# Weight sums stored one stage late, first raw words beside the first layer's last pieces, sums behind Pool's remainders, early differences on VectorE

## The chip, the cores and the metric

The kernel runs on one core of one Trainium2 chip. The metric is the device time of one execution in microseconds. The trace is one execution taken by the hardware profiler; "Pool" and POOL are GpSimd, DVE is VectorE, ACT is ScalarE, PE is TensorE, and SP is the engine whose queue issues every DMA of this kernel.

## The reference, cut to what matters

Attention over 4 batches, 8 heads, 576 positions and 64 features, joined with a memory read-out, then two feed-forward layers, all in float32. The weights arrive as float64, and the kernel gets them as pairs of 32-bit words.

```python
scores = where(causal, -1e9, q @ k.T / sqrt(64))
a = softmax(scores)
local = a @ v
phi = where(q > 0, q, exp(q) - 1) + 1
mem_out = (phi @ M_prev) / (phi @ z_prev + 1e-6)
x = g * mem_out + (1 - g) * local          # g = sigmoid(beta), 2304 tokens x 512

h = x @ w_in                               # layer 1: 512 -> 2048
x = (h * cos(h)) @ w_out                   # 2048 -> 512

h = x @ w2_in                              # layer 2
out = (h * tanh(softplus(h))) @ w2_out
```

## The kernel before, in words

Every operand of a large product is split into a high half (float32r) and a remainder, so that one product is three matmuls: high with high, high with remainder, remainder with high. The functions `split` and `halves` make these pairs of activations: the high half is a copy (L130, a helper, mostly on ScalarE), the remainder a subtraction (L400 in layer 1, L680 in layer 2, mostly on Pool).

The program runs in four stretches of time.

1. **Head and attention with layer 1, first half** (0 to 391 us). `attention` walks 16 head pairs of 5 query blocks each, 80 steps. For each pair `prep` loads q, k, the memory, v and q again (L218 to L229) into rings whose sizes stand in `BUFS` (`kd` 4, `qd` 3, `mb` 2, `vt` 2, `qt` 1). `stage_a` makes scores and the exponential; L279, on Pool, scales the rows; `stage_b` transposes them (L312); `stage_c` multiplies with v (L339). From step 14 on one step also converts pieces of the first layer's weights from raw words (`to_f32`, L143 to L147; remainder L183), and from batch 1 on units of layer 1 with 256 tokens (L428, L494) are put between.
2. **The rest of layer 1** (391 to about 700 us), with 512 tokens at a time in its second half (`m2` in the main loop, L901 to L918). Beside it the main loop converts the other half of the first layer's weights (generator `gb`, the pieces counted by `done_b`) and prepares the second layer.
3. **Layer 2** (from about 668 us, overlapping the end of layer 1, to about 1036 us), `strassen_ffn`: the 2 x 2 block product is made with seven products (names A11, A12, S1 to S4, A22). The sums of weight blocks for this are made beforehand by `strassen_weights`: raw words are fetched three ahead and converted, four sums or differences are made in `sw` (L560, Pool), each of seven is split into `ws` (L130 and L566, by turns on DVE and Pool), and stored to the DRAM tensors `wsD` and `woD` (L567). It runs as generator `gi` for the first 6 of 16 pieces beside the attention (from step `SUM0 - AHEAD` = 29, one call a step) and as `gc` for the other 10 beside the second half of layer 1 (one or two calls per step `i` of the main loop, one on each `SUM2`th).
   In each of 24 groups the products of inputs (L771) alternate with those of outputs of earlier groups (L744); `last_products` runs over a chain of (group pair, name), loads its weights two turns ahead (L620, tile `w`), and `done` adds the result (L710) to one of 14 accumulators. At the end of each of three token blocks `done` combines accumulators (`pre`, L704, and L721, by turns DVE and Pool, kind `yf`) and stores them (L708).
4. **The tail** (1036 us to the end): the last products, sums and stores of the third token block.

Three things set the order around the change. Every DMA is issued from SP's queue in program order, so one that waits for its data or its buffer holds all behind it. The engines run their instructions in order. And a scheduler writes that order when the program is built: it takes the buffers, the dependences and the marks of `tc.issue_after(x)` ("not before x in the order") into account. So a change of a buffer count or of a mark moves instructions everywhere, on engines which the diff does not name too.

Of the kernel before, what the change touches and what calls it, by code (L numbers as in the profile page):

```python
# [9 lines left out]
F32 = mybir.dt.float32  # L10
# [4 lines left out]
ALU = mybir.AluOpType  # L15
# [5 lines left out]
BUFS = dict(  # L21
    mb=2, kd=4, qd=3, aD=4, vt=2, qt=1, ph=2, den=2, mo=4, xH=1, xL=3, sm=7, mn=2, at=8, aT=7, u=2, e=3, g=4, h=4, y=4, xb=3, xbH=4, xbL=4, yp=3, wst=4, S=6, T=8, sw=1, ws=2, wq=10, xr=4, xt=2, xc=10, xc0=2, us=14, g3=17, y3=5, h3=3, w2=8, ac=14,
)
# [3 lines left out]
AHEAD = 3  # L27
SUM0 = 32
SUMS = 6
SUM2 = 3  # L30
XSUM0 = 37
# [9 lines left out]
    sc="p", ws="p", w0l="pv", w1l="vp", w2l="vp", gl="p", gh="v", bh="a", mh="a",  # L41
    wh="ap", aT="av", yl="p", ml="p", y0="v", y1="a", aD="v", y3="a", yf="vp", mz="vp", x3l="v", x3l0="pv", x3d0="p", x3d="v", ws4="p", ws2="a", wh2="a",
)
# [7 lines left out]
def attention_moe_moe_kernel(  # L51
# [14 lines left out]
    nc = tc.nc  # L66
    P = 128
# [10 lines left out]
    NTL = NFH // 2  # L78
# [317 lines left out]
    def split(g, cast, kind):  # L396
        gg = wk.tile([P, 2, SM], F32R, tag="g", name="g", bufs=BUFS["g"])
        gH, gL = gg[:, 0], gg[:, 1]
        scaled(cast, gH, g)
        turn_of(kind).tensor_tensor(gL, g, gH.bitcast(F32), ALU.subtract)  # L400
        return gH, gL
# [142 lines left out]
    def strassen_weights(pieces):  # L544

        raws = ahead([src for srcs, _, _ in pieces for src in srcs])
        for _ in range(AHEAD):
            next(raws)
            yield
        for _, order, dst in pieces:  # L550
# [12 lines left out]
            for k0, k1, t in ((0, 2, pc[1]), (2, 3, pc[0][:, 0:1]), (3, 5, sw[:, :2]), (5, 7, sw[:, 2:])):  # L563
                ws = wk.tile([P, 2, 2, 2, P], F32R, tag="ws", name="ws", bufs=BUFS["ws"])[:, :k1 - k0]
                scaled("wh2", ws[:, :, 0], t)
                turn_of("w2l").tensor_tensor(ws[:, :, 1], t, ws[:, :, 0].bitcast(F32), ALU.subtract)  # L566
                nc.sync.dma_start(dst[:, k0:k1], ws.rearrange("p k l c f -> p k (l c f)").bitcast(F32))  # L567
                yield

    def strassen_x(t0, out, store=False):  # L570
# [67 lines left out]
    def strassen_ffn(pool, xs, w, fill):  # L638
# [6 lines left out]
        acc = {}  # L645
        w2 = {}
        chain = [(k, name) for k in range(0, n, KS) for name in LAST]
        g3 = [wk.tile([P, 2, TS], F32R, tag=f"g3{i}", name="g3", bufs=1) for i in range(BUFS["g3"])]
# [8 lines left out]

        def sub(x, y, out=None, vector=True):
            if out is None:
                out = cell()  # L660
            if vector:
                marks['v'] = nc.vector.tensor_tensor(out, x, y, ALU.subtract).ins  # L662
            else:
                marks['p'] = nc.gpsimd.tensor_tensor(out, x, y, ALU.subtract).ins
            return out
# [23 lines left out]

        def done(k0, name, c, y):  # L690

            t0, tl = groups[k0]
            r = groups[k0][0]
            if tl == 0:
# [7 lines left out]
            def pre(n, other, op=ALU.add):  # L702
                x = acc[n, c]
                turn_of("yf").tensor_tensor(x, *((other, x) if op == ALU.subtract else (x, other)), op)  # L704

            def store(x, e, h):
                e = (2 * e + c) * P
                nc.sync.dma_start(out[e:e + P, t0 + h * TS:t0 + (h + 1) * TS], x)  # L708

# [9 lines left out]
            elif name == "S2":  # L719
                pre("S3", a)  # L720
                turn_of("yf").tensor_tensor(a, a, acc["S1", c], ALU.add)  # L721
                pre("S4", a)
# [8 lines left out]
        def last_products():  # L731
# [3 lines left out]
            for i, (k0, name) in enumerate(chain):  # L735
                fetch_last(i + 2)
                ws = w2.pop(i)
                xs = [g.pop((k, name)) for k in range(k0, k0 + KS)]
                for c in range(2):
                    y = pool.tile([P, SM], F32, tag="y3", name="y", bufs=BUFS["y3"])[:, :TS]  # L740
                    m = 0
                    for w_, (_, x) in zip(ws, xs):
                        for wl, xl in ((0, 0), (0, 1), (1, 0)):
                            nc.tensor.matmul(y, w_[:, wl, c], x[:, xl], start=m == 0, stop=m == 3 * KS - 1,  # L744
                                             skip_group_check=True)
                            m += 1
                    done(k0, name, c, y)
                    if c == 1:
# [13 lines left out]
        for k in range(n + KS):  # L762
# [45 lines left out]
            if k < n:  # L808
                product(C, "S4", False)
                c12 = add(C, u2)  # L810
                r12 = act(c12, c12)
                t1 = sub(r12, r11)
                halves(k, "S1", t1)
                t2 = sub(r22, t1)
                halves(k, "S2", t2)
                halves(k, "S3", sub(r22, r12, r12, k + 1 == n))
                halves(k, "A22", sub(t2, r21, r21, k + 1 == n))
                w = nw
# [42 lines left out]
    for kind, s in at:  # L861
# [5 lines left out]
        if kind == "a" and s >= SUM0 - AHEAD:  # L867
            with tc.issue_after(marks["act"]), tc.issue_after(marks["pool"]), tc.issue_after(marks["vec"]):
                next(gi, None)
        if kind != "c":  # L870
# [28 lines left out]
    with tc.issue_after(marks["sp"]):  # L899
        i = 0  # L900
        while True:  # L901
            while done_b < min(4 * ((i + 2) // 4 + 1), 4 * NTL) - 1:
                with tc.issue_after(marks["cos"]), tc.issue_after(last_sin[0]):
                    done_b = next(gb)
            if next(m2, None) is None:
                break
            i += 1
            if done_b == 4 * NTL - 1:
                with tc.issue_after(marks["cos"]), tc.issue_after(last_sin[0]):
                    for _ in range(1 if i % SUM2 == 0 else 2):  # L910
                        next(gc, None)
# [79 lines left out]
```

## Time and profile before

| what | us |
|---|---|
| median of 3 runs | 1061.12 |
| the three runs | 1054.95, 1061.12, 1062.19 |
| the profiled execution's own time | 1057.27 |
| its span, first to last instruction | 1055.5 |
| PE busy in it | 1017.3 |

The difference between the profiled execution's time and its span, 1.8 us, lies around the instructions. A view of waits lists an engine's idle time by the instruction that came after it and by what released that; a view of windows gives each engine's busy time in a stretch, the granted TensorE clock as a share of full speed, and the busy share and rate of the 16 DMA engines.

### The profile page before, as it was taken

How to read it: one execution, taken by the hardware profiler on the slowest of the kernel's cores; microseconds unless marked ns; L12 is line 12 of the kernel's file. 1: busy time of each engine (PE TensorE's matmuls, PEld its weight loads, DVE VectorE, ACT ScalarE, POOL GpSimd, SP SyncE). 2: the span in 40 equal slices, each digit the busy share in tenths (PEclk: the TensorE clock that was granted, in tenths of full speed). 3: DMA queues.
4: the chain of work that ended last, by engine and by line, in shares of the span. 5: the costliest groups of instructions: out<-in, count | busy, mean ns of one | idle time of the engine just before them, and what ended most of it. 6: DMA issues, size and time to landing. Idle time of an engine off the chain costs nothing.

```text
span 1055.5 us, 19374 instructions
## 1 busy us (share of the span) xinstructions
PE 1017.3 (96%) x6704; PEld 897.9 (85%) x6704; DVE 673.5 (64%) x1400; ACT 576.1 (55%) x1274; POOL 634.7 (60%) x623
## 2 busy tenths in 40 slices
PE   6998999999999999999999989998999999999997
PEld 4665678887878889998887878898999899999996
DVE  3589866667565645885495876453597347962557
ACT  5787576758576653334365555456444454445441
POOL 3368754454444533555386687279677767786664
PEclk8999799999999999999999999999999999999999
DMA  7377554636342247435268989996977888797882
GB/s 255 130 217 243 176 196 145 208 100 232 120 166 104 80 146 269 160 101 170 98 236 291 325 298 335 406 329 246 380 268 256 262 289 293 237 310 237 276 282 80
DMA packets 121841, 236.19 MB, mean 224 GB/s; under 512 B 11920, under 2 KB 35984, under 8 KB 121744
## 3 DMA queue, kind: packets, MB, share of 16 engines
q1 hardware_dynamic: 121744, 234.95, 65.2%
q8 instruction: 54, 0.88, 0.3%
q14 instruction: 43, 0.35, 0.1%
HBM read 176.44 MB, written 58.46 MB: 223 GB/s over the span
## 4 chain that ended last, share of the span: by engine, by line
PE 67%; DMA 9%; DVE 9%; ACT 6%; POOL 4%; issue 4%; SPq 1%; POOLq 0%; ACTq 0%; DVEq 0%
PE y L744 15%; PE h L771 15%; PE h L428 12%; PE y L494 11%; PE o L339 4%; PE sp L252 4%; PE tp L312 3%; DMA wst<-in_w1i_dram 2%; DMA wst<-in_w1o_dram 2%; PE o L328 1%; DVE wst L146 1%; DMA w<-woD 1%; DMA wsD<-ws 1%; POOL at L279 1%; DMA woD<-ws 1%
## 5 line engine op out<-in xcount | busy, mean ns | idle before, releaser
L494 PE MATMUL y<-g,w 128*128 128x256 f32 (+1 forms) x1344 | 222.4, 318 | 4.9 <-POOL g L400 3.9
L680 POOL TENSOR_TENSOR g<-us,g 128x384 fp32r<-128x384 f32 x164 | 177.3, 1099 | 74.2 <-ACT g L130 73.0
L494 PEld LDWEIGHTS y<-g,w 128*128 128x128 f32 x1344 | 191.3, 190 | 33.5 <-issue 10.3
L428 PE MATMUL h<-xbH,w 128*128 128x256 f32 (+1 forms) x896 | 206.5, 318 | 0.6 <-DMA xbH<-xsH 0.6
L744 PE MATMUL y<-g,w 128*128 128x384 f32 x1008 | 196.2, 336 | 4.0 <-DMA w<-woD 2.5
L771 PE MATMUL h<-xc,wq 128*128 128x384 f32 x1008 | 195.7, 335 | 2.6 <-ACT us L786 2.5
L279 POOL TENSOR_SCALAR at<-at,sm,omg 128x128 f32<-128x128 f32 (+2 forms) x144 | 114.3, 802 | 115.2 <-DVE sm L277 68.0
L744 PEld LDWEIGHTS y<-g,w 128*128 128x128 f32 x1008 | 175.9, 188 | 7.2 <-DMA w<-woD 2.4
L771 PEld LDWEIGHTS h<-xc,wq 128*128 128x128 f32 x1008 | 176.2, 188 | 3.4 <-ACT us L786 2.8
L400 POOL TENSOR_TENSOR g<-u,g 128x512 fp32r<-128x512 f32 x72 | 103.3, 1449 | 111.7 <-ACT g L130 54.5
L428 PEld LDWEIGHTS h<-xbH,w 128*128 128x128 f32 x896 | 151.3, 192 | 12.9 <-DMA xbH<-xsH 1.0
L428 PE MATMUL h<-xbL,w 128*128 128x256 f32 (+1 forms) x448 | 141.3, 316 | 0.0
L669 DVE TENSOR_TENSOR us<-h,us 128x384 f32<-128x384 f32 x120 | 66.3, 554 | 109.6 <-PE h L771 78.7
L130 ACT ACTIVATE g<-us 128x384 fp32r<-128x384 f32 x168 | 86.4, 523 | 57.1 <-DVE us L662 29.9
L428 PEld LDWEIGHTS h<-xbL,w 128*128 128x128 f32 x448 | 85.9, 192 | 5.3 <-issue 0.3
L673 ACT ACTIVATE us<-us 128x384 f32<-128x384 f32 x72 | 37.6, 524 | 96.1 <-DVE us L669 96.1
L257 ACT ACTIVATE at<-at,mn 128x128 f32<-128x128 f32 (+3 forms) x128 | 71.0, 556 | 26.1 <-DVE mn L254 24.4
L382 ACT ACTIVATE u<-h 128x512 int32<-128x512 f32 x72 | 42.0, 591 | 71.1 <-PE h L428 70.9
L710 DVE TENSOR_TENSOR ac<-y,ac 128x384 f32<-128x384 f32 x120 | 63.8, 550 | 22.1 <-PE y L744 21.7
L254 DVE CUSTOM_DVE_ANT_0 at<-sp,mask 128x128 f32<-128x128 f32 (+3 forms) x128 | 59.5, 483 | 25.5 <-PE sp L252 20.5
L312 PE MATMUL tp<-ident,at 128*128 128x128 f32 x384 | 65.5, 289 | 9.6 <-POOL at L279 6.0
L383 DVE SCALAR_TENSOR_TENSOR u<-u,h 128x512 f32<-128x512 int32 x72 | 48.3, 679 | 39.5 <-ACT u L382 39.4
(106 smaller groups left out, 1561.5 us busy)
## 6 DMA issues: line engine op xcount, KB each, us to landing
wq<-wsD SPq DMA_DIRECT2D x168, 256.0 KB, 4.5
w<-woD SPq DMA_DIRECT2D x168, 256.0 KB, 4.7
wsD<-ws SPq DMA_DIRECT2D x24, 512.0 KB, 3.2
woD<-ws SPq DMA_DIRECT2D x24, 512.0 KB, 4.4
wst<-in_w1i_dram SPq DMA_DIRECT2D x16, 512.0 KB, 4.5
wst<-in_w1o_dram SPq DMA_DIRECT2D x16, 512.0 KB, 4.8
wst<-in_w2i_dram SPq DMA_DIRECT2D x16, 512.0 KB, 4.5
wst<-in_w2o_dram SPq DMA_DIRECT2D x16, 512.0 KB, 5.2
```

Source lines behind the costliest of these rows:

```text
L130: eng.activation(dst, src, AF.Copy, scale=scale)
L257: marks["act"] = nc.scalar.activation(at[:, :N], at[:, :N], AF.Exp, bias=mn[:, j:j + 1], scale=-1.0, accum_out=sm[:, j:j + 1]).ins
L279: marks["pool"] = turn_of("sc", b == 0).tensor_scalar(at[:, :N], at[:, :N], sm[:, j:j + 1], gates[j], ALU.mult, ALU.mult).ins
L312: nc.tensor.transpose(tp[:, c:c + P], at[:, c:c + P], ident)
L400: turn_of(kind).tensor_tensor(gL, g, gH.bitcast(F32), ALU.subtract)
L428: nc.tensor.matmul(h[:, a * T:(a + 1) * T], w_[:, c, f0:f0 + P], x_[c], start=m == 0, stop=m == 3 * NC - 1)
L494: nc.tensor.matmul(y[e // per][:, cols], w_[:, f, es], g_, start=fst and m == 0 and e % per == 0, stop=lst and m == 2, skip_group_check=True)
L669: marks['v'] = nc.vector.tensor_tensor(c, b, x, ALU.add).ins
L680: ins = turn_of("ml" if k + 1 < n else "mz").tensor_tensor(t[:, 1], x, t[:, 0].bitcast(F32), ALU.subtract).ins
L710: marks['v'] = nc.vector.tensor_tensor(a, *((a, y) if less else (y, a)), ALU.subtract if less else ALU.add).ins
L744: nc.tensor.matmul(y, w_[:, wl, c], x[:, xl], start=m == 0, stop=m == 3 * KS - 1, skip_group_check=True)
L771: nc.tensor.matmul(b, w[name][:, wl, c], x[name][:, xl, c], start=first and m == 0, stop=m == 5, skip_group_check=True)
```

## The change

Eight edits. (1) `qd`, the ring of loaded q, has 4 buffers in place of 3; `ws` has 3 in place of 2. (2) `strassen_weights` keeps each store in a list and issues it after the next stage's split. (3) `gi` starts six steps later (step 35) and makes two calls on every fifth step. (4) `gc` begins earlier: the last three pieces of the first layer's weights are converted on steps 2, 3 and 4 of the main loop and not all on step 10, and `gc` makes a call with each, which are its three first fetches of raw words; from then on it makes two calls on every second step and one on the others (before, two on two of three). (5) Those calls are also marked to come after the last remainder of layer 1 (`marks["gl"]`). (6) The stores of the output are put in a list and issued two turns of the chain later; in the last group pair at once. (7) In the third token block all accumulator sums go to VectorE (kind `yz`). (8) The differences S3 and A22 of groups 0 and 1 go to VectorE, as those of the last group did; the others stay on Pool.

```diff
-... qd=3 ... ws=2 ...
+... qd=4 ... ws=3 ...
-SUM0 = 32
+SUM0 = 38
-SUM2 = 3
+SUM2 = 2
+    ... yz="v" ...
...
-        turn_of(kind).tensor_tensor(gL, g, gH.bitcast(F32), ALU.subtract)
+        marks["gl"] = turn_of(kind).tensor_tensor(gL, g, gH.bitcast(F32), ALU.subtract).ins
...
+        made = []
...
-                nc.sync.dma_start(dst[:, k0:k1], ws.rearrange("p k l c f -> p k (l c f)").bitcast(F32))
+                made.append((dst[:, k0:k1], ws.rearrange("p k l c f -> p k (l c f)").bitcast(F32)))
+                if len(made) > 1:
+                    nc.sync.dma_start(*made.pop(0))
                 yield
+        for m in made:
+            nc.sync.dma_start(*m)
...
-            r = groups[k0][0]
+            turns = "yf" if t0 + 2 * TS < NT else "yz"
...
-                turn_of("yf").tensor_tensor(x, *((other, x) if op == ALU.subtract else (x, other)), op)
+                turn_of(turns).tensor_tensor(x, *((other, x) if op == ALU.subtract else (x, other)), op)
...
-                nc.sync.dma_start(out[e:e + P, t0 + h * TS:t0 + (h + 1) * TS], x)
+                stores.append((turn + 2, out[e:e + P, t0 + h * TS:t0 + (h + 1) * TS], x))
...
                 fetch_last(i + 2)
+                while stores and stores[0][0] <= i:
+                    nc.sync.dma_start(*stores.pop(0)[1:])
...
+                    while stores and k0 + KS == n:
+                        nc.sync.dma_start(*stores.pop(0)[1:])
...
+                eng = nc.gpsimd if KS <= k < n - 1 else nc.vector
...
-                halves(k, "S3", sub(r22, r12, r12, k + 1 == n))
-                halves(k, "A22", sub(t2, r21, r21, k + 1 == n))
+                halves(k, "S3", sub(r22, r12, r12, eng))
+                halves(k, "A22", sub(t2, r21, r21, eng))
...
-                next(gi, None)
+                for _ in range(2 if s % 5 == 0 else 1):
+                    next(gi, None)
...
-            while done_b < min(4 * ((i + 2) // 4 + 1), 4 * NTL) - 1:
+            while done_b < min(max(4 * ((i + 2) // 4 + 1), 4 * NTL - 4 + i), 4 * NTL) - 1:
                 with tc.issue_after(marks["cos"]), tc.issue_after(last_sin[0]):
                     done_b = next(gb)
+                if done_b >= 4 * NTL - 1 - AHEAD:
+                    next(gc)
...
-                with tc.issue_after(marks["cos"]), tc.issue_after(last_sin[0]):
-                    for _ in range(1 if i % SUM2 == 0 else 2):
+                with tc.issue_after(marks["cos"]), tc.issue_after(last_sin[0]), tc.issue_after(marks["gl"]):
+                    for _ in range(2 if i % SUM2 == 0 else 1):
                         next(gc, None)
```

The scheduled order moves with it. On Pool, at the passage from layer 1 to layer 2 (`sw` and `ws` are sums of weights, L400 remainders of layer 1, L680 and L664 remainders and differences of layer 2), the kernel before has

```order
L400 TENSOR_TENSOR g<-u,g 128x512 x4
L566 TENSOR_TENSOR ws<-sw,ws 128x2x256
L680 TENSOR_TENSOR g_7862<-us,g_7862 128x384
L560 TENSOR_TENSOR sw<-wst 128x256 x2
L680 TENSOR_TENSOR g_7863<-us,g_7863 128x384
L560 TENSOR_TENSOR sw<-sw,wst 128x256
L560 TENSOR_TENSOR sw<-wst,sw 128x256
L680 TENSOR_TENSOR g_7864<-us,g_7864 128x384
L664 TENSOR_TENSOR us<-us 128x384
```

and the changed one (L561 and L567 are the old L560 and L566, L682 the old L680) has

```order
L561 TENSOR_TENSOR sw<-wst,sw 128x256
L589 TENSOR_TENSOR xc<-xr,xc 128x768
L400 TENSOR_TENSOR g<-u,g 128x512 x2
L567 TENSOR_TENSOR ws<-wst,ws 128x256
L567 TENSOR_TENSOR ws<-sw,ws 128x2x256
L400 TENSOR_TENSOR g<-u,g 128x512 x6
L682 TENSOR_TENSOR g_7862<-us,g_7862 128x384
L682 TENSOR_TENSOR g_7863<-us,g_7863 128x384
L682 TENSOR_TENSOR g_7864<-us,g_7864 128x384
```

All weight sums stand ahead of layer 2's first remainder, and the remainders of layer 1 stand in pairs. On SP, at the end of the first token block of layer 2 (`wq` and `w` are weights for inputs and outputs), the kernel before has

```order
L708 DMA out_dram<-ac 128x384
L620 DMA wq<-wsD 128x512 x2
L620 DMA w_9535<-woD 128x512
L620 DMA w_9537<-woD 128x512
L708 DMA out_dram<-ac 128x384 x3
L620 DMA wq<-wsD 128x512
L708 DMA out_dram<-ac 128x384
L620 DMA wq<-wsD 128x512
L708 DMA out_dram<-ac 128x384
L620 DMA wq<-wsD 128x512
L620 DMA w_9604<-woD 128x512
L620 DMA w_9606<-woD 128x512
```

and the changed one (L625 is the old L620, L740 the old L708) has

```order
L740 DMA out_dram<-ac 128x384
L625 DMA wq<-wsD 128x512
L625 DMA w_9531<-woD 128x512
L625 DMA w_9533<-woD 128x512
L740 DMA out_dram<-ac 128x384 x3
L625 DMA wq<-wsD 128x512 x3
L625 DMA w_9600<-woD 128x512
L625 DMA w_9602<-woD 128x512
```

The stores stand later against the sums that they wait for, and no store lies between the last loads of `wq` ahead of a pair of `w`. On SP in the head, from the load of the first batch's third pair on, the kernel before has

```order
L220 DMA qd<-in_qT_dram 128x640
L218 DMA kd<-in_kT_dram 128x576
L223 DMA mz<-in_mbd_dram 128x130
L229 DMA qt<-in_qp_dram 128x576
L223 DMA mz<-in_mbd_dram 128x130
L229 DMA qt<-in_qp_dram 128x576 x2
L226 DMA vt<-in_vn_dram 128x640
L346 DMA xsH<-xH 128x576
```

and the changed one has

```order
L220 DMA qd<-in_qT_dram 128x640
L218 DMA kd<-in_kT_dram 128x576
L223 DMA mz<-in_mbd_dram 128x130
L220 DMA qd<-in_qT_dram 128x640
L218 DMA kd<-in_kT_dram 128x576
L229 DMA qt<-in_qp_dram 128x576
L223 DMA mz<-in_mbd_dram 128x130
L229 DMA qt<-in_qp_dram 128x576
L226 DMA vt<-in_vn_dram 128x640
L346 DMA xsH<-xH 128x576
```

One more pair's q and k are loaded ahead of the first store of the attention's result.

## Rows read from the trace of the kernel before

**Rows 1.** The page: granted TensorE clock in 40 slices, in tenths.

```profile
PEclk8999799999999999999999999999999999999999
```

**Rows 2.** Windows by stretch: busy us (instructions), granted clock, DMA share, GB/s.

```profile
0.00:120.00 120.00, 103.86 (x712) 68.98 (x713) 84.30 (x291) 86.44 (x262) 73.06 (x98) 0.89 0.66 213
120.00:391.00 271.00, 267.41 (x2242) 219.82 (x2241) 170.43 (x520) 176.56 (x437) 127.02 (x145) 1.00 0.44 146
391.00:668.00 277.00, 273.32 (x1581) 241.13 (x1580) 188.63 (x228) 130.10 (x207) 164.32 (x133) 1.00 0.67 235
668.00:1036.00 368.00, 361.10 (x2116) 357.64 (x2116) 214.64 (x336) 179.58 (x361) 261.62 (x241) 1.00 0.82 283
1036.00:1056.00 20.00, 11.62 (x62) 10.29 (x60) 15.53 (x27) 3.39 (x7) 8.69 (x8) 0.91 0.30 106
```

**Rows 3.** PE's waits, 416 to 668 us: total us, times, longest us.

```profile
PE y L494 <- POOL g L400: 3.0, 3, 1.7
```

**Rows 4.** PE's waits, 668 us to the end.

```profile
PE y L744 <- DMA w<-woD: 2.5, 2, 2.1
PE h L771 <- ACT us L786: 2.5, 1, 2.5
PE y L494 <- POOL g L400: 0.9, 1, 0.9
PE y L744 <- POOL g L680: 0.5, 1, 0.5
```

**Rows 5.** Timeline around 608 us: start, us, engine, line, operation [idle before].

```profile
605.77 2.57 POOL L605 TENSOR_TENSOR xr<-xr 128x768 f32<-128x768 f32 x1
...
608.31 1.71 POOL L400 TENSOR_TENSOR g<-u,g 128x512 fp32r<-128x512 f32 x1
...
610.08 2.81 PE L494 MATMUL y<-g,w 128*128 128x512 f32 x11 [1.15 <-POOL g L400]
```

**Rows 6.** Windows of line L560 alone: busy of POOL.

```profile
680.00:745.00 65.00, 6.75 (x8) 1.00 0.85 308
```

**Rows 7.** Windows of line L566 alone: busy of DVE, then POOL.

```profile
680.00:745.00 65.00, 4.59 (x4) 6.58 (x5) 1.00 0.85 308
```

**Rows 8.** Timeline of DVE, 700 to 746 us.

```profile
719.38 0.56 DVE L669 TENSOR_TENSOR us<-h,us 128x384 f32<-128x384 f32 x1 [4.30 <-POOL g L680]
```

**Rows 9.** Timeline of PE, 716 to 727 us.

```profile
725.52 1.66 PE L771 MATMUL h<-xc,wq 128*128 128x384 f32 x8 [2.47 <-ACT us L786]
```

**Rows 10.** Timeline of SP, 800 to 836 us (issues).

```profile
820.15 3.45 SPq L708 DMA_DIRECT2D out_dram<-ac  x3
...
826.40 2.23 SPq L620 DMA_DIRECT2D w<-woD  x2
```

**Rows 11.** Timeline of PE, 826 to 836 us.

```profile
832.28 0.79 PE L744 MATMUL y<-g,w 128*128 128x384 f32 x3 [2.12 <-DMA w<-woD]
```

**Rows 12.** SP's own waits: total us, times, longest us.

```profile
SPq L567 <- DVE ws L566: 93.4, 22, 12.0
...
SPq L567 <- POOL ws L566: 54.8, 18, 11.5
...
SPq L220 <- PE sd L265: 20.8, 7, 6.3
...
SPq L708 <- DVE ac L710: 10.8, 6, 6.5
```

**Rows 13.** Timeline of DVE, 1040 us to the end.

```profile
1044.24 1.48 DVE L710 TENSOR_TENSOR ac<-y,ac 128x384 f32<-128x384 f32 x3
...
1051.56 0.56 DVE L710 TENSOR_TENSOR ac<-ac,y 128x384 f32<-128x384 f32 x1
```

**Rows 14.** Timeline of POOL, 1040 us to the end.

```profile
1045.80 1.26 POOL L704 TENSOR_TENSOR ac<-ac 128x384 f32<-128x384 f32 x1 [2.47 <-DVE ac L710]
...
1048.52 3.78 POOL L704 TENSOR_TENSOR ac<-ac 128x384 f32<-128x384 f32 x3 [0.49 <-DVE ac L721]
```

**Rows 15.** POOL, line L664: duration ns min/median/max, first and last start.

```profile
L664 POOL TENSOR_TENSOR us<-us x46: 1004/1017/1739, 698.4 to 1025.6; 128x384 f32<-128x384 f32 x46
```

**Rows 16.** Windows in the head, columns as in rows 2.

```profile
60.00:100.00 40.00, 35.24 (x265) 23.20 (x263) 36.55 (x111) 31.36 (x95) 33.03 (x36) 0.91 0.70 218
100.00:120.00 20.00, 18.12 (x105) 11.56 (x104) 16.67 (x48) 12.07 (x37) 17.76 (x22) 0.68 0.76 247
```

More of the change, by code (lines that the diff above doesn't have):

```diff
@@ L21 @@
 BUFS = dict(
-    mb=2, kd=4, qd=3, aD=4, vt=2, qt=1, ph=2, den=2, mo=4, xH=1, xL=3, sm=7, mn=2, at=8, aT=7, u=2, e=3, g=4, h=4, y=4, xb=3, xbH=4, xbL=4, yp=3, wst=4, S=6, T=8, sw=1, ws=2, wq=10, xr=4, xt=2, xc=10, xc0=2, us=14, g3=17, y3=5, h3=3, w2=8, ac=14,
+    mb=2, kd=4, qd=4, aD=4, vt=2, qt=1, ph=2, den=2, mo=4, xH=1, xL=3, sm=7, mn=2, at=8, aT=7, u=2, e=3, g=4, h=4, y=4, xb=3, xbH=4, xbL=4, yp=3, wst=4, S=6, T=8, sw=1, ws=3, wq=10, xr=4, xt=2, xc=10, xc0=2, us=14, g3=17, y3=5, h3=3, w2=8, ac=14,
 )
@@ L41 @@
     sc="p", ws="p", w0l="pv", w1l="vp", w2l="vp", gl="p", gh="v", bh="a", mh="a",
-    wh="ap", aT="av", yl="p", ml="p", y0="v", y1="a", aD="v", y3="a", yf="vp", mz="vp", x3l="v", x3l0="pv", x3d0="p", x3d="v", ws4="p", ws2="a", wh2="a",
+    wh="ap", aT="av", yl="p", ml="p", y0="v", y1="a", aD="v", y3="a", yf="vp", yz="v", mz="vp", x3l="v", x3l0="pv", x3d0="p", x3d="v", ws4="p", ws2="a", wh2="a",
 )
@@ L646, in strassen_ffn @@
         w2 = {}
+        stores = []
         chain = [(k, name) for k in range(0, n, KS) for name in LAST]
@@ L656, in cell, with sub @@
             return wk.tile([P, TS], F32, tag="us", name="us", bufs=BUFS["us"])
[L658 to L664, printed above, removed]
+        def sub(x, y, out=None, eng=nc.vector):
+            out = cell() if out is None else out
+            marks['v' if eng is nc.vector else 'p'] = eng.tensor_tensor(out, x, y, ALU.subtract).ins
             return out
@@ L688, in fetch_last, with done @@
                     w2[i] = [load_w(groups[k][1], name, "w2", woD) for k in range(k0, k0 + KS)]
-        def done(k0, name, c, y):
+        def done(turn, k0, name, c, y):
             t0, tl = groups[k0]
-            r = groups[k0][0]
+            turns = "yf" if t0 + 2 * TS < NT else "yz"
             if tl == 0:
@@ L720, in done @@
                 pre("S3", a)
-                turn_of("yf").tensor_tensor(a, a, acc["S1", c], ALU.add)
+                turn_of(turns).tensor_tensor(a, a, acc["S1", c], ALU.add)
                 pre("S4", a)
@@ L746, in last_products @@
                             m += 1
-                    done(k0, name, c, y)
+                    done(i, k0, name, c, y)
+                    while stores and k0 + KS == n:
+                        nc.sync.dma_start(*stores.pop(0)[1:])
                     if c == 1:
```

## The prediction, made before the run

> **What bounds the kernel now.** I read the windows by stretch first. TensorE is busy 103.86 of 120 us in the head, and from 120 us on for 267.41 of 271, 273.32 of 277 and 361.10 of 368 us; VectorE, ScalarE and Pool have idle time everywhere after the head [rows 2]. So from 120 to 1036 us the kernel is a row of matmuls with 14.2 us of holes (3.6, 3.7 and 6.9), and outside of that stand 16.1 us of holes in the head and 8.4 us at the end. A change that leaves the matmuls as they are can win only holes, or a half-speed clock: the granted clock is under nine tenths in the first and the fifth slice alone, up to 132 us [rows 1]. The second view is that of TensorE's waits by stretch, which names each hole, and the third the timelines around the largest, which say who came late. SP's own waits come last: they look large (93.4 and 54.8 us behind the splits of weight sums [rows 12]), but a waiting queue costs only where TensorE waits for a transfer behind it.
>
> **The change part by part, against the profiled execution (1057.27 us, span 1055.5).**
>
> *Sums behind Pool's remainders (edit 5).* TensorE waits for a remainder of layer 1 on Pool three times for 3.0 us before 668 us and once for 0.9 after [rows 3, 4]. One of them can be followed: Pool runs a 2.57 us difference of the input sums, then the remainder of 1.71, and the matmuls come 1.15 us late [rows 5]. In the changed order the two remainders of a unit stand together, with the sums behind them. Gain between 0 (something else is late just there) and 3.9; I take 3.0, because all four waits name the same line, and the order moves for all of it. If the cover goes, a late remainder costs what the row shows, 1 to 1.7 us each.
>
> *Sums finished before layer 2 (edits 2, 4 and the third `ws` buffer).* From 680 to 745 us, inside layer 2, the last sums still take 6.75 + 6.58 us of Pool and 4.59 of VectorE [rows 6, 7]. There Pool's remainders hold the cells that VectorE's adds need: an add waits 4.30 us for one [rows 8], and TensorE then 2.47 us for the bank behind it [rows 9]; 0.5 us more waits for Pool directly [rows 4]. The changed order has every sum ahead of layer 2's first remainder on Pool, so these 3.0 us should go: bounds 0 and 3.0, I take 3.0. The work comes back before 668 us, where Pool is busy 164.32 and VectorE 188.63 of 277 us [rows 2]; 13.3 us more on Pool make 178, still under two thirds, and calls that were on steps after 10 now start at step 2. Hence I cost the work itself at nothing. If it isn't hidden, it delays remainders as the four in rows 3 and 4 were, so the loss is bounded by about as much again, 3.9 us. The later stores themselves are the same transfers; SP waits for a split 40 times now (148 us in all [rows 12]) and mostly won't, and the loads of raw words behind them come earlier. TensorE waits for none of these, so they enter with 0.
>
> *Stores of the output two turns later (edit 6).* Three stores hold SP from 820.15 for 3.45 us, SP waits 10.8 us for accumulators in all [rows 10, 12], the pair of `w` is issued only at 826.40, and TensorE waits 2.12 us for it at 832.28 [rows 11]. With a smaller wait of the same kind that is 2.5 us [rows 4]. After the change the accumulators are done when their stores come up. Bounds 0 (the transfers, not the queue, are late: the DMA engines are busy 82% here [rows 2]) and 2.5; I take 2.3.
>
> *All sums of the third block on VectorE (edit 7).* From 1044.24 us to the end of the last instruction (1051.56 + 0.56 = 1052.12) 17 sums run, 12 on VectorE and 5 on Pool, in 7.88 us [rows 13, 14]. On VectorE alone at 0.49 (1.48 for three) to 0.56 us each [rows 13] they take 8.3 to 9.5 us, and VectorE never waits for Pool. Pool needs 1.26 us for one [rows 14], so the split bought little. I take a loss of 1.0; bounds 1.6 lost, and 1 gained if the chain between the two engines was what held it.
>
> The Trainium skill (Perfetto Trace Analysis, Optimizing Scalar/DVE Operations) says that GpSimd and VectorE share a read port, "so offloading operations between those two might not help". By that rule edits 7 and 8 would both be worth 0, and the sum 1.0 better; the tail's rows agree that two engines together were hardly faster than one.
>
> *Early differences on VectorE (edit 8).* Four of Pool's 1.017 us instructions [rows 15] go to an engine that is busy 214.64 of 368 us [rows 2]. With the sums gone Pool no longer holds anybody there; 0, bounded by the 0.5 us that TensorE waits for L680 [rows 4] either way.
>
> *A fourth `qd`, and `gi` six steps later (edits 1, 3).* They reorder the attention from its first pair on, and the trace of before does not show that order. From 60 to 120 us TensorE is idle for 6.6 us, and the clock stands at 0.91 and then 0.68 [rows 16], so 7.2 and 12.8 us were at the half level; at most 10 us of that were lost to it. Gain at most 16.6. Loss: the 53.4 us of work, done at a mean of 0.83, would take 65.4 us if all of it ran at 0.68: 12 us. SP waits 20.8 us for q's buffer in the whole attention [rows 12], and one more buffer takes most of it, but the memory's and v's buffers stay as they were, and VectorE, busy 53.2 of these 60 us, stays what the stretch waits for. The sums that begin later free VectorE and Pool between about 130 and 175 us, where TensorE has part of its 3.6 us of holes. I take a gain of 2.0, near nothing against both ends.
>
> **Sum:** 3.0 + 3.0 + 2.3 - 1.0 + 2.0 = 9.3, so 1057.27 - 9.3 = 1048.0. The profiled execution stands 3.9 below the median of the three runs, which spread over 7.2; the mean of all four is 1058.9, 1.6 above the profiled one. I add that: 1049.6, or 11.5 below the median shown. A measurement of this kernel can tell about 1% from no change, so "faster" begins at 1050.5.
>
> **The rivals.**
>
> *A. The head gets better too.* For it: the loads run one pair ahead, and in the changed order one more pair's q and k precede the first store. Against: VectorE sets that stretch. If half of the 16.6 us go, the sum is 6.3 better: 1043.
>
> *B. The holes only move.* For it: the DMA engines are busy 82% in layer 2, and the sums are put into a stretch whose end already had long waits; the scheduler moved everything, so other remainders and loads can be late. Against: Pool and VectorE are far from full between 391 and 668 us. If of the 8.3 us taken in the three late terms 6.5 come back as other waits: 1056.
>
> *C. Slower, by the head's clock.* The conversions of weights from 60 us on keep VectorE so full that TensorE starves; the granted clock of 0.68 follows a stretch in which TensorE was idle for 4.8 of 40 us [rows 16]. If TensorE uses its attention work up earlier, since q is there earlier, it has less to fill that stretch, and the clock stays at 0.68 throughout: 12 us lost in place of 2 won, 1063.6. It decides as soon as the head loses more than 7.3, what the other terms win. With the three late gains failing as well it is 1071.9.
>
> *D. The change doesn't do what it says* holds for the stores alone: if what held them was the DMA engines, the 2.3 us stay, 1052. It lies within the forecast's own range.
>
> **How the numbers follow.** Forecast 0.50, with 1045 to 1055 around it, of which 0.27 lie below 1050.5; A 0.20, all faster; B 0.18 (0.02 faster, 0.15 the same, 0.01 slower); C 0.12 (0.05 the same, 0.07 over 1% slower, with the late gains failing too). That gives faster 0.49, the same 0.43, slower 0.08. The range goes from 1038, with most of A, to 1064, with the milder half of C.
>
> **What would show it.** Right: no wait of TensorE for L400, no weight sums after the first remainder of layer 2, no wait of 2 us at the first token block's end, and 368 us of layer 2 shorter by about 5; the last VectorE instruction about a microsecond later after the last matmul than now. Wrong: a head of 120 us that has moved by more than 5, either way, or new waits for `wq`, `w` or raw words between 560 and 740 us as large as those that went.

## The result, and the profile after

The changed kernel takes 1047.47 us (median of 6 runs, 1046.26 to 1049.16); the kernel before took 1061.65 beside it (6 runs, 1054.83 to 1065.04). The ratio is 0.9882 with a 95% interval of 0.9844 to 0.9920: faster by 0.8 to 1.6%. The forecast of 1049.6 was 2.1 us too high. The profiled execution took 1047.30 us, span 1045.5, so 10.0 below the one of before. The medians differ by 14.2 us: the traces below explain the 10.0, and the rest lies in slower executions of the kernel before, of which there is no trace.

The first view to read is windows, with bounds at which both kernels have done the same number of matmuls (within two), and with the last bound at the last matmul's end. The kernel before (us; busy us and instructions of PE, PEld, DVE, ACT and POOL; granted clock; DMA share; GB/s):

```profile
0.00:178.40 178.40, 159.86 (x1193) 114.93 (x1193) 126.66 (x415) 126.14 (x360) 102.64 (x128) 0.92 0.60 195
178.40:740.00 561.60, 552.38 (x3767) 480.47 (x3766) 350.19 (x673) 309.96 (x633) 312.88 (x297) 1.00 0.60 211
740.00:1048.40 308.40, 305.07 (x1749) 302.45 (x1747) 193.07 (x309) 139.96 (x283) 215.40 (x196) 1.00 0.79 266
```

The changed kernel:

```profile
0.00:172.40 172.40, 151.88 (x1193) 112.98 (x1193) 122.85 (x409) 123.28 (x354) 103.09 (x127) 0.95 0.60 197
172.40:730.00 557.60, 549.17 (x3765) 479.64 (x3764) 351.29 (x677) 310.80 (x632) 308.03 (x290) 1.00 0.62 215
730.00:1038.40 308.40, 305.38 (x1751) 302.79 (x1749) 202.67 (x318) 142.75 (x289) 214.71 (x195) 1.00 0.79 263
```

So 6.0 us are won by the 1193rd matmul, 4.0 between it and the first fifth of layer 2 (3.6 where the matmuls are counted one by one), half a microsecond at most in the 1750 matmuls after that, and nothing in the tail (7.1 us to the end of the span in both). In the first stretch PE is busy 8.0 us less, but idle 2.0 us *more* (20.5 for 18.5): what shrank is busy time, the half-level clock's among it (27.3 us before, 17.1 after), not the holes.

The head, whose rows of before are [rows 16], and the two long stretches that answer to [rows 2]:

```profile
60.00:100.00 40.00, 33.21 (x240) 22.69 (x237) 35.46 (x104) 31.01 (x93) 37.82 (x39) 0.96 0.75 239
100.00:120.00 20.00, 16.31 (x137) 12.60 (x139) 19.38 (x55) 14.50 (x43) 17.22 (x18) 0.88 0.59 191
...
391.00:668.00 277.00, 270.82 (x1560) 238.44 (x1559) 195.12 (x234) 134.47 (x219) 175.26 (x146) 1.00 0.71 251
668.00:1036.00 368.00, 365.01 (x2138) 362.74 (x2137) 224.51 (x351) 176.26 (x354) 246.66 (x224) 1.00 0.80 269
```

From 60 to 120 us the clock rose from 0.91 and 0.68 to 0.96 and 0.88. Work moved forward: Pool is busy 175.26 us from 391 to 668 us, where it was 164.32, and 246.66 from there to 1036 us, where it was 261.62. TensorE's waits of the changed kernel from 391 to 668 us (us, times, longest), against [rows 3]:

```profile
PE y L494 <- POOL g L400: 3.6, 3, 1.7
PE y L494 <- DVE yp L517: 1.3, 1, 1.3
PE h L428 <- DMA xbH<-xsH: 1.3, 2, 0.7
```

and from 668 us to the end, against [rows 4]; these two are all there are:

```profile
PE y L748 <- DMA w<-woD: 2.2, 2, 1.7
PE y L748 <- POOL g L682: 0.8, 1, 0.8
```

The remainders (L400) are late as before, and a late load of x and a late sum of the layer's output (L517) have joined them. In layer 2 the wait of 2.5 us for L786 is gone. The wait for `w` is there as before.

### The profile page after: what moved, and what is told of

Its sections match the earlier page's. It is cut to its first block, busy times and chain, and to the rows that moved or that the text cites. A ratio compares the mean times of both kernels' runs of the same rounds, so it can differ in the third digit from the quotient of the medians.

```text
span 1045.5 us, 19409 instructions
## 1 busy us (share of the span) xinstructions
PE 1006.4 (96%) x6704; PEld 895.4 (86%) x6704; DVE 680.9 (65%) x1411; ACT 576.8 (55%) x1274; POOL 625.8 (60%) x612
## 4 chain that ended last, share of the span: by engine, by line
PE 76%; DMA 7%; DVE 6%; ACT 3%; POOL 3%; issue 3%; SPq 1%; DVEq 0%; POOLq 0%; ACTq 0%
PE y L494 16%; PE h L777 15%; PE h L428 15%; PE y L748 15%; PE o L339 4%; PE tp L312 3%; PE sp L252 3%; PE o L328 1%; PE mp L292 1%; DMA qd<-in_qT_dram 1%; DMA wst<-in_w1o_dram 1%; DMA xbH<-xsH 1%; POOL at L279 1%; DMA w<-woD 1%; ACT u L387 1%
## 5 line engine op out<-in xcount | busy, mean ns | idle before, releaser
L682 POOL TENSOR_TENSOR g<-us,g 128x384 fp32r<-128x384 f32 x164 | 180.3, 1117 | 99.6 <-ACT g L130 96.3
L400 POOL TENSOR_TENSOR g<-u,g 128x512 fp32r<-128x512 f32 x72 | 103.1, 1449 | 112.5 <-ACT g L130 47.4
L147 DVE SCALAR_TENSOR_TENSOR wst<-wst 128x512 int32<-128x512 int32 x64 | 73.8, 1165 | 0.3
L312 PE MATMUL tp<-ident,at 128*128 128x128 f32 x384 | 63.4, 284 | 8.3 <-POOL at L279 5.3
L390 DVE TENSOR_TENSOR u<-h,u 128x512 f32<-128x512 f32 x72 | 46.3, 685 | 36.4 <-ACT u L387 36.4
```

The costliest lines, as they stand in the source:

```text
L147: nc.vector.scalar_tensor_tensor(lo, hi, 3, lo, ALU.logical_shift_left, ALU.bitwise_or)
L312: nc.tensor.transpose(tp[:, c:c + P], at[:, c:c + P], ident)
L400: marks["gl"] = turn_of(kind).tensor_tensor(gL, g, gH.bitcast(F32), ALU.subtract).ins
L682: ins = turn_of("ml" if k + 1 < n else "mz").tensor_tensor(t[:, 1], x, t[:, 0].bitcast(F32), ALU.subtract).ins
```

## The experiments

Each ratio is against the kernel before on the same chip, with its 95% interval; the table sorts them by what they answer. The last two columns are of the profiled execution alone: when the 1193rd matmul starts, and how long it is from there to the start of the last one (us). The kernel before stands at 178.4 and 869.7, the changed one at 172.4 and 865.7. For `e6_warm` its 126 added matmuls are left out of the count.

| run | what it is | median us (range, runs) | ratio | 1193rd at | rest |
|---|---|---|---|---|---|
| e1_head_only | before + edits 1 (`qd` alone) and 3 | 1051.16 (1049.58 to 1055.01, 7) | 0.9933 [0.9908, 0.9959] | 174.2 | 867.7 |
| e10_qd_only | before + `qd` | 1053.08 (1047.56 to 1056.09, 10) | 0.9933 [0.9905, 0.9961] | 173.4 | 867.5 |
| e5_no_qd | changed - `qd` | 1055.46 (1048.51 to 1057.64, 10) | 0.9946 [0.9916, 0.9975] | 180.2 | 866.1 |
| e6_warm | before + junk matmuls | 1061.11 (1056.82 to 1065.80, 10) | 1.0018 [0.9988, 1.0048] | 186.3 | 869.9 |
| e2_gc_only | before + edit 4 | 1056.34 (1053.21 to 1058.57, 10) | 0.9981 [0.9960, 1.0001] | 175.8 | 870.0 |
| e7_no_gc_gl | changed - edits 4, 5 | 1047.70 (1046.12 to 1049.04, 4) | 0.9889 [0.9841, 0.9937] | 172.7 | 864.2 |
| e8_no_ws | changed - third `ws` | 1052.07 (1048.77 to 1056.29, 10) | 0.9929 [0.9904, 0.9954] | 172.9 | 872.6 |
| e9_no_late | changed - edit 2 | 1046.68 (1046.47 to 1047.90, 4) | 0.9878 [0.9836, 0.9920] | 172.2 | 865.1 |
| e3_no_late_out | changed - edit 6 | 1047.49 (1046.40 to 1048.43, 4) | 0.9889 [0.9859, 0.9920] | 173.3 | 865.0 |
| e4_no_yz | changed - edit 7 | 1048.93 (1047.48 to 1049.05, 4) | 0.9904 [0.9868, 0.9939] | 172.4 | 865.6 |
| e11_w3 | e7 + output weights a turn earlier | 1054.03 (1050.04 to 1055.73, 12) | 0.9932 [0.9909, 0.9956] | 172.1 | 873.5 |
| e12_w3_xd | changed + that + differences on DVE | 1054.04 (1051.52 to 1058.43, 12) | 0.9941 [0.9918, 0.9964] | 175.7 | 872.9 |

### The head: which edit, and is it the clock?

```diff
-    ... qd=3 ...
+    ... qd=4 ...
-SUM0 = 32
+SUM0 = 38
-                next(gi, None)
+                for _ in range(2 if s % 5 == 0 else 1):
+                    next(gi, None)
```

> The kernel before with only the fourth buffer of q and the later, uneven calls of gi; the sums of weights still stand inside layer 2. Theory (the traces): the head gives over half of the whole gain, because the granted clock stands at the lower level for about 10 us in place of 20 between 60 and 132 us. At equal matmul work the kernel is 5 to 6 us ahead of before from 140 us on and gains nothing later: about 1055.5 where before has 1061, ratio 0.9945; layer 2 again begins with a wait of 2 to 3 us for L786. Rival (the prediction): the head gives 2.0 us, ratio 0.998, and the rest comes from the late stretches.

More than half of the whole gain (0.0067 of 0.0118) came with the head's two edits. The wait for L786, expected at 2 to 3 us again, is 0.6 us, though the sums of weights still stand inside layer 2 (17.3 us of L560 and L566 from 680 to 745 us). `e10_qd_only` then has the buffer alone:

```diff
-    ... qd=3 ...
+    ... qd=4 ...
```

> The kernel before with a fourth buffer of q alone. Theory (q's buffer carries the head): the gain of the run with q's buffer and gi together, 0.993 to 0.995. Rival (gi's later start has a part in it): half of that, 0.997.

One buffer gives 0.9933 too, so nothing of `gi` can be told from nothing. The converse, in the changed kernel:

```diff
-    ... qd=4 ...
+    ... qd=3 ...
```

> The changed kernel with three buffers of q, as before; the order of the head's first 200 rows on TensorE is again that of before. Theory: the head's gain goes and the late one stays: 1051 to 1053, ratio 0.993, with 17 us or more at the lower clock between 60 and 135 us. Rival: the gain of the head belongs to the later calls of gi, not to q's buffer: ratio 0.988 as the changed kernel.

It lost 8.0 us of medians. Its windows:

```profile
0.00:60.00 60.00, 51.33 (x317) 34.41 (x319) 27.56 (x123) 39.00 (x119) 20.10 (x40) 0.86 0.54 181
60.00:132.00 72.00, 65.72 (x468) 45.70 (x464) 63.22 (x183) 52.54 (x157) 58.68 (x62) 0.83 0.67 214
```

The same stretches of the kernel before are

```profile
0.00:60.00 60.00, 50.50 (x348) 34.22 (x350) 31.09 (x134) 43.01 (x132) 22.26 (x42) 0.94 0.59 197
60.00:132.00 72.00, 63.97 (x472) 43.77 (x469) 63.58 (x182) 51.76 (x153) 56.75 (x61) 0.86 0.67 210
```

The clock is low from 60 us on, as it was before, but the first 60 us are worse here than in the kernel before, which has as many buffers. So a part of what this trace lost belongs to the start of its execution. For the timed runs the ratios, 0.9946 to 0.9882, give 6.8 us.

To separate the clock from the order, `e6_warm` adds three products of the identity, overwritten at once, ahead of each tile's transposes in steps 18 to 29, to keep TensorE busy there:

```diff
+                if 18 <= (b * NP + p) * NQ + i < 30:
+                    for _ in range(3):
+                        nc.tensor.matmul(tp[:, :P], ident, ident, start=True, stop=True)
```

> The kernel before with three matmuls of the identity ahead of the transposes of each tile in steps 18 to 29 (their result is overwritten by the transposes): some 66 matmuls of 0.11 us, 7 us more work for TensorE in the stretch in which it idles. Theory 1 (the lower clock itself costs the time): it stands lower for under 10 us between 60 and 135 us, and the first matmul of layer 1, at 118.0 us before, comes 2 us or more earlier in spite of the added work. Theory 2 (TensorE's idle time and its clock are only signs, VectorE and the conversions set the stretch): the first matmul of layer 1 comes at 118 us or up to 7 later, whatever the clock does.

```profile
0.00:60.00 60.00, 50.89 (x316) 34.01 (x316) 27.31 (x122) 38.73 (x117) 20.12 (x40) 0.86 0.54 180
60.00:132.00 72.00, 68.19 (x568) 52.19 (x566) 57.53 (x174) 50.05 (x145) 51.40 (x54) 0.98 0.67 210
```

From 60 to 132 us the clock stood at 0.98 in place of 0.86, and yet nothing was won: the first matmul of layer 1 started at 132.5 us (118.0 before). The profiled execution also lost 4.7 us ahead of the edited steps, as its first 60 us show; by the 1193rd matmul, the added ones left out, it stands 7.9 us behind the kernel before. Neither theory's number came out. A full clock here isn't enough for a gain; whether the low clock in the kernel before was a cause or a sign of the starved stretch stays open.

The timed runs bear on it too. In the 70 executions of the kernel before that were timed beside these twelve kernels, on three chips, the time falls by 7 to 8 us for each 0.01 of the mean granted clock (correlation -0.62 to -0.86), and lines through them give 1057.0 to 1057.5 us at 0.988. The changed kernel's six executions, at 0.988 to 0.991, took 1046.26 to 1049.16. So some 10 us of the gain stand at an equal clock, and the clock goes with 2 to 3 us more. This is a correlation, and no run sets the clock alone.

### The passage to layer 2: which edit?

Edit 4 alone in the kernel before:

```diff
-SUM2 = 3
+SUM2 = 2
-            while done_b < min(4 * ((i + 2) // 4 + 1), 4 * NTL) - 1:
+            while done_b < min(max(4 * ((i + 2) // 4 + 1), 4 * NTL - 4 + i), 4 * NTL) - 1:
+                if done_b >= 4 * NTL - 1 - AHEAD:
+                    next(gc)
-                    for _ in range(1 if i % SUM2 == 0 else 2):
+                    for _ in range(2 if i % SUM2 == 0 else 1):
```

> The kernel before with only the other calls of gc (first ones on steps 2 to 4, then two on every second step); head and attention in the same order as before. Theory: the passage to layer 2 alone gives 3 to 4.5 us, ratio 0.996 to 0.997, since the wait for L786 and the 4.3 us of the add behind Pool go; head as before within 1 us. Rival: those waits belong to the third buffer and the late stores, and the earlier calls alone leave the waits at 720 us or move them to 560 to 660 us: ratio 1.000.

The wait for L786 went, as expected, but loads of x came late instead. Its waits of TensorE from 391 to 668 us:

```profile
PE h L428 <- DMA xbH<-xsH: 2.7, 2, 2.3
PE y L494 <- POOL g L400: 1.7, 2, 1.2
PE h L428 <- DMA xbL<-xsL: 0.8, 1, 0.8
```

The ratio, 0.9981, takes in no change, and the rest after the 1193rd matmul takes 870.0 us for 869.7: the wait that went bought nothing there.

The opposite, the changed kernel with this diff undone and without the mark `gl`:

> The changed kernel with gc's calls on the steps of before and without the mark behind Pool's remainders; the third buffer and the late stores stay. Head and attention are in the changed kernel's order. Theory (the earlier calls alone moved the waits and won nothing, so the third buffer with late stores carries the passage to layer 2): the time is within 1.5 us of the changed kernel, ratio 0.989. Rival: the calls and the mark carry it: 4 us slower, ratio 0.992, with a wait of 2 us or more for L786.

It is as fast as the changed kernel: 1047.70 and 1047.47. Edits 4 and 5 are worth nothing measurable. Of what is left at this place, `e8_no_ws` takes the third buffer away:

```diff
-    ... ws=3 ...
+    ... ws=2 ...
```

> The changed kernel with two buffers of ws, as before; late stores, gc's calls and the mark stay. Theory (the third buffer carries it): 3 to 5 us slower than the changed kernel, ratio 0.992, with loads of xb or remainders late between 550 and 700 us as in the run with gc's calls alone. Rival (two suffice): within 1 us, ratio 0.988.

and `e9_no_late` the late stores of sums:

```diff
-                made.append((dst[:, k0:k1], ws.rearrange("p k l c f -> p k (l c f)").bitcast(F32)))
-                if len(made) > 1:
-                    nc.sync.dma_start(*made.pop(0))
+                nc.sync.dma_start(dst[:, k0:k1], ws.rearrange("p k l c f -> p k (l c f)").bitcast(F32))
```

> The changed kernel with each weight sum's store issued at once, as before; the third buffer of ws, gc's calls and the mark stay. TensorE's order is the changed kernel's, row for row. Theory (the third buffer alone carries it): within 1 us of the changed kernel, ratio 0.988 to 0.989. Rival (the late store is needed, as SP would wait for each split with loads of xb behind it): 2 us slower or more, with waits for xb above 2.5 us.

The buffer carries it: without it 4.6 us are lost; without the late stores, nothing. In the profiled executions the loss lies behind the 1193rd matmul, 872.6 us for 865.7. That is 2.9 more than in the kernel before, which has two buffers as well (this execution is 2.6 above its own median). So a part of the buffer's price may be what the other edits cost without it; the third buffer alone in the kernel before wasn't tried. TensorE's waits of `e8_no_ws`, 391 to 668 us:

```profile
PE h L428 <- DMA xbH<-xsH: 4.0, 3, 3.1
PE y L494 <- POOL g L400: 2.5, 3, 1.4
```

and ScalarE's, over the span, ahead of its copies of high halves into `ws`:

```profile
ACT ws L130 <- DMA woD<-ws: 22.1, 10, 7.9
ACT ws L130 <- DMA wsD<-ws: 12.6, 7, 4.3
```

against the changed kernel's

```profile
ACT ws L130 <- DMA woD<-ws: 10.4, 6, 4.2
...
ACT ws L130 <- DMA wsD<-ws: 2.2, 2, 1.5
```

With two buffers a copy waits until a store of an earlier sum has landed, 34.7 us in all; with three, 12.6. (In the kernel before, with two and the calls as they were, it was 20.9.) The loads of x, which stand behind these stores on SP, are late in the same run, which fits; that link wasn't tested by itself.

### The output's stores, and the tail

```diff
-                stores.append((turn + 2, out[e:e + P, t0 + h * TS:t0 + (h + 1) * TS], x))
+                nc.sync.dma_start(out[e:e + P, t0 + h * TS:t0 + (h + 1) * TS], x)
```

> The changed kernel with the stores of the output issued at once, as before. Theory (the traces): they were worth nothing, since the wait for w stands at 2.2 us in the changed trace as against 2.5; the time is the changed kernel's within 0.5 us, ratio to before 0.988. Rival (the prediction): the stores held SP and cost 2.3 us: ratio 0.990, with a wait for w of 4 us or more in all.

No difference (1047.49), and the profile's wait for `w` was even smaller, 0.9 us. In the changed kernel SP's issues at the first token block's end are

```profile
813.67 1.32 SPq L740 DMA_DIRECT2D out_dram<-ac  x3
815.08 1.49 SPq L625 DMA_DIRECT2D wq<-wsD  x3
816.62 0.90 SPq L625 DMA_DIRECT2D w<-woD  x2
818.25 1.36 SPq L625 DMA_DIRECT2D wq<-wsD  x2
819.66 1.50 SPq L625 DMA_DIRECT2D w<-woD  x2
```

The stores are issued without a wait among them, and still the last pair of `w` is issued at 819.66, behind loads of `wq`, and TensorE waits 1.72 us for it at 822.71. For the tail, the third block's sums go by turns to VectorE and Pool again:

```diff
-            turns = "yf" if t0 + 2 * TS < NT else "yz"
-                turn_of(turns).tensor_tensor(x, *((other, x) if op == ALU.subtract else (x, other)), op)
+                turn_of("yf").tensor_tensor(x, *((other, x) if op == ALU.subtract else (x, other)), op)
```

> The changed kernel with the third block's sums by turns on VectorE and Pool, as before. The order is the same up to the tail. Theory (the traces: 4.1 us from the last matmul's end to VectorE's last instruction as against 3.8): ending 0.3 us earlier, which no timing can tell. Rival 1 (the prediction): 1.0 us earlier. Rival 2: 0.5 us later or more, since the chain between the two engines was what held it.

1048.93, inside the range of the changed kernel.

### Two attempts at a better version

The output weights loaded three turns ahead and not two, on the version of `e7_no_gc_gl`; then the same on the changed kernel, with the last two differences of layer 2's first input sums (L610, L612) on VectorE (the last line of the edit, in `e12_w3_xd` alone):

```diff
-            for i in range(2):
+            for i in range(3):
-                fetch_last(i + 2)
+                fetch_last(i + 3)
-    ... x3d0="p" ...
+    ... x3d0="v" ...
```

> The changed kernel without gc's other calls and the mark, and with the output weights loaded three turns of the chain ahead in place of two, in the same 8 buffers. Theory (the pair of w comes late because it is issued late, behind loads of wq that wait for their buffers): the waits for w, 1.5 us in the run without gc's calls and 2.2 in the changed kernel, go to under 0.5, and the time is 1 to 2 us under the changed kernel's, ratio 0.987. Rival (the 16 DMA engines are full there): the waits stay, ratio 0.989.

> The changed kernel with the output weights loaded three turns ahead, and the last two differences of the first input sums (L610, L612 of the changed kernel) on VectorE and not on Pool, where they stand just ahead of a pair of remainders. Theory (these differences, and not the sums, are what the remainders of layer 1 still wait for): the waits for L400, 3.6 us, fall under 1.5 and those for w under 0.5, together 3 to 4 us under the changed kernel's time, ratio 0.985. Rival: VectorE, busy 195 of 277 us there, delays other work in their place: ratio 0.989.

Both are slower than the changed kernel, by 6.6 us of medians. In their profiled executions the loss lies in layer 2: from the 4958th matmul (at 730.5 us in the changed kernel) to the last they take 314.0 and 315.6 us, and the changed kernel 307.5. So it goes with the third turn, which both have; what in it costs the time wasn't traced. `e11_w3` still waits 3.1 us for `w` once. `e12_w3_xd` has no wait for L400 left, which its theory said, but from the 1193rd to the 4958th matmul it is only 0.8 us ahead of the changed kernel (557.3 for 558.1), since others came in their place. From 391 to 668 us:

```profile
PE h L428 <- DMA xbH<-xsH: 2.6, 2, 2.0
PE y L494 <- DVE yp L517: 1.9, 1, 1.9
```

and from 668 us on:

```profile
PE h L777 <- DVE us L671: 3.5, 2, 1.8
PE h L777 <- ACT us L675: 1.4, 2, 0.7
PE y L748 <- DMA w<-woD: 1.0, 2, 0.6
```

No version tried beats the changed kernel.

## Why the prediction was right, and where its terms were wrong

The total was right, 9.3 us against 10.0 in the profiled executions, but by luck, since it was put together from the wrong terms: what the head won above its term (4.0 us) and the tail's loss that did not come (1.0) made up for the 4.3 us by which the three late terms fell short (4.0 for 8.3). Of the prediction's own signs for being right the one on the sums came (none after the first remainder of layer 2). L400 is still waited for, and layer 2 from the 4958th matmul on is 0.5 us shorter, not about 5.

**Head (2.0 taken, 6.0 measured).** The step that failed is "VectorE, busy 53.2 of these 60 us, stays what the stretch waits for", and with it the choice of a value near nothing: VectorE is as full there in the changed kernel (54.8 of 60 us), and the head moved all the same. The term also priced 60 to 120 us alone and put the first 60 at nothing without a reason, where 3.7 of the 6.0 us were won: the 348th matmul starts at 56.3 us and not at 60.0, at 55.7 to 58.0 in all ten traces with four buffers of q and at 60.0 to 64.6 in the four with three. Rival A, half of the 16.6 us, or 8.3 in the head, was nearer; its condition, one more pair's loads ahead of the first store, is what happened, and a head moved by more than 5 was the prediction's own sign against its step. The last score of the fifth pair starts at 71.5 us (86.1 before), and the time at half level (1.2 of 2.4 GHz) falls from 27.3 to 17.1 us. But SP's wait for q's buffer (L220), which I thought the buffer would take away, did not fall: 26.0 us for 20.8 [rows 12]. What fell is SP's wait in the first 60 us for VectorE to release `qt`, a ring of one buffer. In the kernel before it is

```profile
SPq L229 <- DVE ph L233: 12.0, 3, 6.7
```

and in the changed one

```profile
SPq L229 <- DVE ph L233: 4.9, 2, 3.1
```

This wait is 11.8 to 17.3 us in the four traces with three buffers of q and 4.1 to 5.1 in the ten with four. In the new order another pair's q and k stand ahead of that waiting load. So the buffer seems to act through the scheduler, which writes another order from the first rows on; no run has that order with three buffers. Rival C fell: the clock between 100 and 120 us rose from 0.68 to 0.88.

**Sums behind Pool's remainders (3.0 taken, 0 shown).** Three waits for L400 stay, 3.6 us. The step that failed is "The gain ... because all four waits name the same line, and the order moves for all of it". What holds a remainder are the input differences of layer 2, which stand directly ahead of it, as [rows 5] had shown for one already. Pool of the changed kernel around 601 us:

```profile
600.52 2.30 POOL L610 TENSOR_TENSOR xr<-xr 128x768 f32<-128x768 f32 x1
602.77 3.41 POOL L400 TENSOR_TENSOR g<-u,g 128x512 fp32r<-128x512 f32 x2
```

The matmuls behind it come 1.62 us late at 604.54. `e12_w3_xd`, which moves these differences, is the run that removes the waits (`e11_w3`, without that move, has 3.8 us of them); `e7_no_gc_gl`, which undoes the order of the sums, changes no time.

**Sums before layer 2 (3.0 taken).** The effect is as predicted: no L560 or L566 work from 680 to 745 us, where there were 17.9 us [rows 6, 7], and no wait for L786. But the step between the two, that the sums' work there makes TensorE wait, failed: `e10_qd_only` has 16.7 us of it in the same window and no wait for L786, and `e2_gc_only` has 2.1 us, no such wait either, and gains nothing that can be told from nothing. The chain from the add of [rows 8] to the 2.47 us was misread as well. Between them, in the kernel before, VectorE waited for ScalarE's copy of a sum and ran that sum's split, and ScalarE, just ahead of L786, waited for what stood behind that on VectorE:

```profile
722.38 1.15 DVE L566 TENSOR_TENSOR ws<-sw,ws 128x512 fp32r<-128x512 f32 x1 [2.43 <-ACT ws L130]
...
724.57 0.52 ACT L130 ACTIVATE g<-us 128x384 fp32r<-128x384 f32 x1 [0.66 <-DVE us L662]
```

The sum of this term and the one before, 6.0, stands against 4.0 in the stretch from the 1193rd matmul to 740 us, and `e8_no_ws` prices the buffer at 4.6. Of the three causes that the prediction named, edits 2 and 4 aren't needed, and the third `ws` is. The second step, "Hence I cost the work itself at nothing", failed in part: L517 and the loads of x now hold TensorE for 1.3 us each. Rival B, that the holes only move, holds for a part of this.

**Late stores of the output (2.3 taken, 0 measured).** The lower bound of this term; the time is rival D's, but its cause, full DMA engines, isn't shown. The step that failed is that the pair of `w` comes late because stores hold SP: with the stores out of the way the pair is again issued late, behind loads of `wq`, and the wait is 2.2 us for 2.5. In the changed kernel SP waits 106.8 us in all for products of inputs to release `wq`, but which of its loads delays this pair wasn't tried alone; loading it a turn earlier made the whole slower.

**Tail (-1.0 taken, 0 to -0.4 measured).** The last sum ends 4.13 us after the last matmul, 3.76 before, so the split on two engines had bought 0.4 us. That lies within the bounds given; the stretch behind the last matmul is 7.1 us in both. The Trainium skill (Perfetto Trace Analysis, Optimizing Scalar/DVE Operations), which says that moving work between GpSimd and VectorE may not help, agrees with `e4_no_yz`, 1048.93 for 1047.47 with ranges that overlap.

**Early differences (0).** Nothing speaks against it, but this edit and the mark of edit 5 weren't tried alone, and no run has `qd` and `ws` without all the rest. By the ratios `qd` is worth 0.0064 to 0.0067 and `ws` 0.0047, together 0.0111 to 0.0114 of 0.0118.

One premise was wrong as well: that only holes or a low clock can be won. From the 1193rd matmul to 740 us PE's idle time fell by 0.8 us only (9.2 to 8.4), and the time by 4.0. Matmuls overlap: those of 384 columns start 173 ns apart, but each is shown for about 335. So a matmul that starts late shows less idle time than it costs, or none. Counted from start to start against the undisturbed distance (120, 173 and 227 ns for 256, 384 and 512 columns), the layers' matmuls were late by about 20 us in this stretch before and by about 16 after, of which about 10 and 9 stood where no idle time is shown at all.

## What to carry to other kernels

When a scheduler writes the order, treat a buffer count as an edit of the whole program: here two numbers, one more buffer for loaded q and one more for finished sums, carried nearly all of the gain by the ratios of the runs without them (the two alone were not run), and six of the other seven edits, left out singly or in a pair, carried none that could be measured. Undo edits one at a time from the faster version, since a sum that comes out right may be made of wrong terms. Before a late instruction is blamed on a kind of work, read what stands directly ahead of it on its engine; and count a wait of pipelined matmuls from start to start.

## What the runs showed of the hardware that was not expected

The first stretch at half level differs between executions of the same order: in the profiled execution of before it lasted from 14.9 to 21.7 us, while in that of `e6_warm`, whose order is the same up to step 18, it lasted 17.1 us, and the second pair's last score came at 39.7 us in place of 35.0. So the same order can lose 4.7 us at its start in one execution, which would be about half of the 10 us over which the kernel before spreads. Of the four traces with three buffers of q two have 17.1 us there and two 6.8; of the ten with four none has more than 6.8. The changed kernel and the four versions of it as fast as it (`e3_no_late_out`, `e4_no_yz`, `e7_no_gc_gl`, `e9_no_late`) spread over 3.0 us in 22 runs; why is not known, since `e10_qd_only`, with four buffers too, spreads over 8.5.
